# Eleven more w2 steps as seven block products: a gated mix of linear attention and an MLP on one core

## The chip, the core and the metric

The kernel runs on one core of one Trainium2 chip. The metric is the device time of one execution in microseconds (us); the three runs shown below took 1128.09 to 1129.79 us. The engines are named as in the profile: PE (matmuls; PEld are its weight loads), DVE (vector), ACT (scalar and activation), POOL (GpSimd) and SP, whose queue issues nearly all DMAs. PE and DVE/ACT meet in PSUM, 8 banks of 128 x 512 fp32.

## The reference

```python
def _A_ref(x, wqkv, wo):                 # linear attention, 32 heads of 18
    ...
    num = jnp.einsum("bhqd,bhde->bhqe", pq, kv)
    den = jnp.einsum("bhqd,bhd->bhq", pq, z)[..., None] + 1e-6
    o = num / den
    return (lambda x, *d: x.transpose(*d))(o, 0, 2, 1, 3).reshape(B, S, D) @ wo
def _B_ref(x, w1, b1, w2, b2):
    y = _layernorm(x, axis=-1)
    h = _gelu(jnp.einsum("bsd,df->bsf", y, w1) + b1)
    return jnp.einsum("bsf,fd->bsd", h, w2) + b2
g = _sigmoid((x * gate_w).sum(-1, keepdims=True))
return g * a + (1 - g) * b               # a = _A_ref(x, ...), b = _B_ref(x, ...)
```

There are S = 2048 tokens, D = 576 and F = 4608, all fp32.

## The kernel before

**Numbers as pairs.** fp32 values are split into a rounded part (type fp32r) and the rest, so that a product of two matrices is three products of parts: high x high, high x low, low x high. ACT makes the high part by a copy into fp32r, DVE the low part by a subtraction. Every split costs one instruction on ACT and then one on DVE.

**Stages.** First come q, k, v and the attention (to about 279 us in the trace), whose weighted result of the tokens 0 to 1023 stays in SBUF (`acc[0..7]`) and that of the tokens 1024 to 2047 goes to DRAM (`late_acc`). Then the MLP runs to the end in 36 steps, k = 0 to 35: 18 for the first 1024 tokens ("first half") and 18 for the others ("second half"). A step takes 256 of the 4608 hidden columns (two blocks f of 128) for 1024 tokens (two groups t of 512). The helper class `InOrder` records every instruction, so all of them carry its line in the profile, L109, and are told apart by their tiles.

**A step, part one: w1.** The product y @ w1 of a step is a 2 x 2 by 2 x 2 block product. It is made with Winograd's seven block products (`product`, tiles `y,wa` and `y,wb`), each of seven matmuls of 128 x 512; 49 matmuls per step. The PSUM banks X, Yb and Z hold sums of products. ACT copies X out (`kept`, u<-ps), DVE adds another bank (`plus`, u<-ps,u), ACT takes gelu twice (once rounded into `h`, once whole into `u`), DVE subtracts (h<-u,h). The w1 blocks and their sums are split in the first half (wa, wb, by ACT and DVE, the sums by POOL) and stored in DRAM (`w1d`); the second half loads them.

**A step, part two: w2.** h @ w2 of step k is done during the products of step k+1. In steps 0 to 17, 34 and 35 it is plain (`down`): eight tiles of 128 tokens, each 12 matmuls of 128 x 288 (two f, three terms, two halves of the columns) into a pair of PSUM banks; DVE then adds the pair, times 1-g, into the attention's result (accs<-ps,omg,accs). In steps 18 to 33 it is done with seven block products too (`unit`): 14 units of 6 matmuls of 128 x 288, each evicted by a DVE addition (accs<-ps,accs) into seven sums that are combined at the end. This asks for sums of h (`sum_h`, four POOL operations u<-u of 128 x 512, each split again by ACT and DVE) and sums of w2 blocks (`sum_w2`, four POOL operations fresh<-fresh of 128 x 288).

**What sets the order.** Each engine takes its instructions in program order. The order is written out by hand: one unit or tile of w2 behind each product or part of a product, with the splits at fixed places between them (`todo`, `later`). The units use two PSUM pairs in turn (`ff_pairs`, banks 6-7 and 4-5), so the unit after the next one waits until this one is evicted. Splitting y of the second half (tiles accs, region, yd) is spread over steps 1 to 15.

Of the kernel before, what the change touches and what calls it, by code (L numbers as in the profile page):

```python
# [17 lines left out]
P = 128  # L18
S, D, H, DH, F = 2048, 576, 32, 18, 4608
NT = S // P  # L20
# [49 lines left out]
A11, A12, S2, S1, A21, A22, S3, S4 = range(8)  # L70
FIRST_W, LAST_W = (A11, S1), (A22, S4)
# [6 lines left out]
PLAIN = 2 * NCHUNK - 2  # L78
LAST = 2 * NCHUNK - 1
DOWN_ORDER = (1, 4, 2, 5, 7, 6, 3)  # L80
W2_PLACES = [FACTORS[n][1] for n in DOWN_ORDER]
W2_GROUPS = ((0, 2), (2, 4), (4, 6), (6, 7))
# [30 lines left out]
def tile_gated_mix(ctx: ExitStack, tc: tile.TileContext, x, xm, xe, wm, we, wvm, wve, wo, um, ue, w2, b1, b2, gw, out):  # L113
# [39 lines left out]
    for _ in range(WARM):  # L153
# [11 lines left out]
    sums = {n: accs[:, i * TPB * HALF:(i + 1) * TPB * HALF].rearrange("p (s n) -> p s n", n=HALF)  # L165
            for i, n in enumerate(DOWN_ORDER)}
# [8 lines left out]
    mrt = keep.tile([2 * max(q1 - q0 for q0, q1 in MOMENTS), P], F32, name="mrt")  # L175
    moments = [dram.tile([2, (q1 - q0) * P], F32, name=f"moments{b}") for b, (q0, q1) in enumerate(MOMENTS)]
    w1d = [dram.tile([P, 7, 5, P], F32, name=f"w1d{c}") for c in range(NCHUNK)]
    late_acc = dram.tile([TPS, P, D], F32, name="late_acc")
# [203 lines left out]
    def store_moments(b, p):  # L382
        n = mr[b].shape[1] * mr[b].shape[2]
        act.activation(mrt[:n], p[:n], AF.Copy)
        sp.dma_start(moments[b].rearrange("a (t n) -> (a t) n", n=P), mrt[:n])
# [35 lines left out]
    def split_pair(sup, j, part, stage):  # L421
        m0, m1 = 2 * part, min(2 * part + 2, 7)
# [316 lines left out]
    for m in (B11, B21, T2, T1, T3, T4, B22):  # L739
        load_y(0, m)  # L740
# [15 lines left out]
    hs, c2s, w2raw = {}, {}, {}  # L756

    def wr(k):
        at_ = fresh[:, :24 * P] if k > 1 else spare[:, :24 * P]
        return at_.rearrange("p (m s n) -> p m s n", m=8, s=3)  # L760
# [9 lines left out]
    def sum_w1(k):  # L770
        r = wr(k)
        for to, x0, x1, op in ((S1, A21, A22, OP.add), (S2, S1, A11, OP.subtract), (S4, A12, S2, OP.subtract),
                               (S3, A11, A21, OP.subtract)):
            pool.tensor_tensor(out=r[:, to], in0=r[:, x0], in1=r[:, x1], op=op)

    def split_w1(k, first):

        a, b = FIRST_W if first else LAST_W
        b += 1
        w = wa if first else wb  # L780
        src = wr(k)[:, a:b]
        act.activation(w[:, :, 0:3], src, AF.Copy)
        dve.tensor_sub(w[:, :, 3:5], src[:, :, 0:2], raw(w[:, :, 0:2]))
        dve.tensor_sub(w[64:P, :, 2], src[64:P, :, 2], raw(w[64:P, :, 2]))
# [8 lines left out]
    def load_split_w1(k, a):  # L793
        place = a if a <= FIRST_W[1] else a - LAST_W[0] + 4
        sp.dma_start(raw(w1_of(a)).rearrange("p s n -> p (s n)"),
                     w1d[k % NCHUNK][:, place].rearrange("p s n -> p (s n)"))

    def w2_rows(k):
        c = k % NCHUNK
        return w2[c * CF * P:(c + 1) * CF * P].rearrange("(f p) d -> p f d", p=P)  # L800

    def load_w2(k, to):
        w2raw[k] = to.rearrange("p (f n) -> p f n", f=CF)
        sp.dma_start(w2raw[k], w2_rows(k))

    def split_w2(k, to, parts=(0, 1)):
        c2 = c2s[k] = to.rearrange("p (a f n) -> p a f n", a=2, f=CF)
        if 0 in parts:
            act.activation(c2[:, 0], w2raw[k], AF.Copy)
        if 1 in parts:  # L810
            dve.tensor_sub(c2[:, 1], w2raw[k], raw(c2[:, 0]))
# [19 lines left out]
    def plus(t, p):  # L831
        dve.tensor_tensor(out=t, in0=p, in1=t, op=OP.add)
        return t

    def gelu(k, f, t, src, whole, h=None, split=True):

        bias = b1s[:, k % NCHUNK * CF + f:k % NCHUNK * CF + f + 1]
        if split:
            h = hs[k, f, t] = take_h((k, f, t)) if h is None else h
            act.activation(h[:, 0], src, AF.Gelu_apprx_tanh, bias=bias)  # L840
        act.activation(whole, src, AF.Gelu_apprx_tanh, bias=bias)
        return lambda: dve.tensor_sub(h[:, 1], whole, raw(h[:, 0]))

    TERMS = ((0, 0), (0, 1), (1, 0))
    terms = [(f, a, w) for f in range(CF) for a, w in TERMS]

    def add(i, to, term):
        dve.scalar_tensor_tensor(to, term, omg[:, PLACE[i]:PLACE[i] + 1], to, op0=OP.mult, op1=OP.add)

    def down_terms(p, s, k, half, only=range(len(terms)), opens=True, closes=True):  # L850
        c0 = s % TPB * P
        for n in only:
            f, a, w = terms[n]
            pe.matmul(p, hs[k, f, s // TPB][:, a, c0:c0 + P], c2s[k][:, w, f, half_cols(half)],
                      start=opens and n == 0, stop=closes and n == len(terms) - 1)

    def down(k, s):

        if k >= 0:
            p = two_of(ff_pairs)[:, :, :HALF]  # L860
            for n in range(len(terms)):
                for half in range(2):
                    down_terms(p[:, half], s, k, half, (n,))
            if s % TPB == TPB - 1:
                give_back_h((k, 0, s // TPB), (k, 1, s // TPB))
            add(s, halves(acc[s]), p)
            if k == 1 + s:
                add(s, acc[s], b2b)
            if k == HALF_TIME - 1:
                sp.dma_start(out[s * P:(s + 1) * P, :], acc[s])  # L870
        for job in later.get((k + 1, s), ()):
            job()
# [3 lines left out]
    b2b = ffc.tile([P, D], F32, name="b2b")  # L876
    wa = ffc.tile([P, FIRST_W[1] - FIRST_W[0] + 1, 5, P], F32R, name="wa")
    wb = ffc.tile([P, LAST_W[1] - LAST_W[0] + 1, 5, P], F32R, name="wb")

# [4 lines left out]
    extra[3] += [lambda: sp.dma_start(b2b, everywhere(b2, D))]  # L884
    extra[5] += [lambda: sum_w1(0), lambda: act.activation(tiny, ones[:, 0:1], AF.Gelu_apprx_tanh)]
    extra[7] += [lambda: split_w1(0, True), lambda: store_w1(0, True)]
    extra[9] += [lambda: split_w1(0, False), lambda: load_w1(1), lambda: store_w1(0, False)]
    extra[11] += [lambda: sum_w1(1)]

# [18 lines left out]
    h_places = ctx.enter_context(tc.tile_pool(name="hp", bufs=1)).tile([P, 6, 2, SB], F32R, name="h")  # L908
    h_free, h_taken = list(range(6)), {}

    def take_h(key):
        h_taken[key] = h_free.pop(0)
        return h_places[:, h_taken[key]]
# [4 lines left out]
    up = ctx.enter_context(tc.tile_pool(name="up", bufs=6))  # L918


    fresh = ctx.enter_context(tc.tile_pool(name="fresh", bufs=1)).tile([P, 33 * P], F32, name="fresh")
    region = ctx.enter_context(tc.tile_pool(name="region", bufs=1)).tile([P, 56 * P], F32R, name="region")
    y_stage = [region[:, n * 10 * P:(n + 1) * 10 * P].rearrange("p (m s n) -> p m s n", m=2, s=5) for n in range(2)]
    w2_whole = fresh[:, 24 * P:33 * P]
    c2_places = [region[:, (20 + 18 * n) * P:(38 + 18 * n) * P] for n in range(2)]
    w2_sums = fresh[:, :7 * HALF].rearrange("p (m n) -> p m n", n=HALF)
# [310 lines left out]
```

## Time and profile before

| | |
|---|---|
| runs | 1129.5, 1129.79, 1128.09 us; median 1129.5 |
| span of the profiled execution | 1127.9 us |
| PE busy | 1116.1 us (99%), 6886 matmuls |
| DVE busy | 862.3 us (76%), 1292 instructions |
| ACT busy | 555.6 us (49%), 950 |
| POOL busy | 308.4 us (27%), 252 |
| DMA | 189.84 MB, mean 168 GB/s |

The profiled execution has no time of its own among the runs; its span, from the first to the last instruction, is 0.2 us below the fastest run and 1.6 us below the median. A row of a timeline gives start, duration, engine, line, operation, out<-in and shapes; matmuls overlap each other, so the pace of PE is read from one start to the next and not from the durations. A row of groups ends with busy time, mean duration in ns, and the idle time before the group with what ended it.

### The profile page before, as it was taken

The numbers are of one execution on the slowest core, as the hardware profiler recorded it, in microseconds if no ns is written. First come the engines' busy times: TensorE is split into PE (matmuls) and PEld (weight loads), VectorE is DVE, ScalarE is ACT, GpSimd is POOL, SyncE is SP. The second block draws the span as 40 slices with busy tenths as digits, with TensorE's granted clock in tenths as the row PEclk, the third lists the DMA queues.
The fourth block names the chain that finished last, engine by engine and source line by source line (L and its number), as shares of the span: only waits on it lengthen the run. The fifth ranks groups of instructions, "written<-read, shape, count | busy, mean of one in ns | idle before, by whom it ended". The sixth has DMA issues, their size and how long they took to land.

```text
span 1127.9 us, 18132 instructions
## 1 busy us (share of the span) xinstructions
PE 1116.1 (99%) x6886; PEld 1022.6 (91%) x6886; DVE 862.3 (76%) x1292; ACT 555.6 (49%) x950; POOL 308.4 (27%) x252
## 2 busy tenths in 40 slices
PE   9999999999999999999999999999999999999998
PEld 8999989999899999999999999988999899989988
DVE  4567775895669878778778765678899889888985
ACT  6667664443545444545444543455444544454441
POOL 2111112342111123112122111234453445344530
PEclk9999999999999999999999999999999999999999
DMA  6267854524454764555755549744444444444452
GB/s 183 58 112 262 174 165 185 232 93 144 172 168 171 230 220 155 210 168 191 241 190 175 189 165 385 292 134 121 123 136 136 122 121 136 136 120 123 137 174 84
DMA packets 102984, 189.84 MB, mean 168 GB/s; under 512 B 8300, under 2 KB 58748, under 8 KB 98674
## 3 DMA queue, kind: packets, MB, share of 16 engines
q1 hardware_dynamic: 102018, 187.94, 51.7%
q8 instruction: 54, 0.88, 0.3%
q10 hardware_dynamic: 720, 0.74, 0.2%
q14 instruction: 32, 0.26, 0.1%
q0 software_dynamic: 160, 0.01, 0.0%
HBM read 121.93 MB, written 66.73 MB: 167 GB/s over the span
## 4 chain that ended last, share of the span: by engine, by line
PE 87%; DVE 6%; ACT 3%; issue 2%; DMA 1%; SPq 0%; ACTq 0%; DVEq 0%
PE ps L109 87%; DVE den L109 1%; DVE accs L109 1%; DVE qt L109 1%; DVE region L109 1%; DVE acc L109 0%; DVE u L109 0%; DMA t<-in_xe 0%; DMA s<-in_we 0%; DMA s<-in_wm 0%; DVE y L109 0%; ACT L109 0%; ACT h L109 0%; ACT u L109 0%; SPq L109 0%
## 5 line engine op out<-in xcount | busy, mean ns | idle before, releaser
L109 PEld LDWEIGHTS ps<-region,h 128*128 128x128 f32 x2568 | 368.5, 188 | 23.1 <-DVE accs L109 1.0
L109 PE MATMUL ps<-region,h 128*128 128x288 f32 x2568 | 383.1, 295 | 0.9 <-DVE fresh L109 0.7
L109 PE MATMUL ps<-y,wa 128*128 128x512 f32 x1008 | 265.0, 392 | 0.0
L109 POOL TENSOR_TENSOR fresh<-fresh 128x384 f32<-128x384 f32 (+1 forms) x128 | 138.1, 1084 | 438.2 <-DMA fresh<-in_ue 175.0
L109 PE MATMUL ps<-y,wb 128*128 128x512 f32 x756 | 201.1, 395 | 1.0 <-ACT u L109 1.0
L109 PEld LDWEIGHTS ps<-y,wa 128*128 128x128 f32 x1008 | 177.8, 188 | 26.2
L109 DVE TENSOR_TENSOR accs<-ps,accs 128x576 f32<-128x576 f32 x210 | 158.0, 753 | 32.3 <-PE ps L109 22.7
L109 ACT ACTIVATE h<-u,b1s 128x512 fp32r<-128x512 f32 x90 | 65.3, 725 | 215.7 <-DVE u L109 215.7
L109 PEld LDWEIGHTS ps<-y,wb 128*128 128x128 f32 x756 | 132.9, 188 | 23.3 <-ACT u L109 1.7
L109 DVE SCALAR_TENSOR_TENSOR accs<-ps,omg,accs 128x576 f32<-128x576 f32 (+1 forms) x146 | 118.1, 810 | 45.0 <-PE ps L109 44.0
L109 ACT ACTIVATE u<-ps 128x512 f32<-128x512 f32 x108 | 63.8, 591 | 149.3 <-PE ps L109 149.0
L109 POOL TENSOR_TENSOR u<-u 128x512 f32<-128x512 f32 x64 | 100.2, 1566 | 126.0 <-ACT u L109 122.2
L109 PE MATMUL ps<-y 128*128 128x288 f32 (+1 forms) x896 | 126.5, 297 | 3.2 <-DVE acc L109 2.0
L109 PEld LDWEIGHTS ps<-y 128*128 128x128 f32 x896 | 122.2, 188 | 6.6 <-DVE acc L109 2.7
L109 DVE TENSOR_TENSOR h<-u,h 128x512 fp32r<-128x512 f32 x142 | 104.8, 738 | 27.3 <-ACT u L109 27.2
L109 ACT ACTIVATE u<-u,b1s 128x512 f32<-128x512 f32 x108 | 78.3, 725 | 53.9 <-DVE u L109 50.9
L109 DVE TENSOR_TENSOR u<-ps,u 128x512 f32<-128x512 f32 x108 | 74.2, 687 | 36.3 <-ACT u L109 23.3
L109 PEld LDWEIGHTS ps<-region 128*128 128x128 f32 x600 | 90.3, 188 | 8.9 <-ACT accs L109 0.5
L109 DVE TENSOR_TENSOR region<-fresh,region 128x576 fp32r<-128x576 f32 (+1 forms) x83 | 80.9, 975 | 20.7 <-ACT region L109 20.7
L109 PE MATMUL ps<-region 128*128 128x288 f32 x600 | 96.2, 295 | 0.1
L109 PE MATMUL ps<-wp,qt 128*128 128x288 f32 x448 | 63.6, 298 | 0.9 <-DVE qt L109 0.9
L109 PEld LDWEIGHTS ps<-wp,qt 128*128 128x128 f32 x448 | 59.9, 188 | 1.4 <-DVE qt L109 1.4
(136 smaller groups left out, 1056.2 us busy)
## 6 DMA issues: line engine op xcount, KB each, us to landing
w1d<-wa SPq DMA_DIRECT2D x18, 1280.0 KB
wa<-w1d SPq DMA_DIRECT2D x72, 320.0 KB
y<-yd SPq DMA_DIRECT2D x14, 1280.0 KB
w1d<-wb SPq DMA_DIRECT2D x18, 960.0 KB
wb<-w1d SPq DMA_DIRECT2D x54, 320.0 KB
fresh<-in_w SPq DMA_DIRECT2D x20, 576.0 KB
fresh<-in_w SPq DMA_DIRECT2D x32, 288.0 KB
fresh<-in_um SPq DMA_DIRECT2D x64, 128.0 KB
```

Of the source, the lines that this page charges most:

```text
L109: return lambda *args, **kwargs: self.tc.keep_in_program_order(op(*args, **kwargs))
```

## The change

- **Which steps.** The list `SEVEN` puts k = 1, 3, ..., 15 and 16 to 34 on seven block products for w2; 0, 2, ..., 14 and 35 stay plain. Before it was 18 to 33.
- **Added straight into the result.** The units run in the order 1, 2, 6, 5, 7, 3, 4 (`DOWN_ORDER`), for tokens q = 0 and then q = 1 of each group. Units 1, 2 and 5 open a PSUM pair; the others add onto what the pair already holds. Every unit is evicted by DVE with one addition into `acc8`, eight tiles of the result. There are no seven sums to combine. The factor 1-g is applied once for each tile at the end of each half (`finish_tile`), so the attention's result of the first half goes to DRAM too and is loaded again.
- **Plain steps.** A unit is 12 matmuls for two token tiles and one half of the columns. For token group t = 0 ACT copies the running result into the PSUM pair ahead of the matmuls (ps<-accs) and copies the pair out behind them (accs<-ps); for t = 1 DVE adds as before.
- **Products.** The order is 1, 5, 6, 2, 7, 4, 3, and ACT copies X into Yb inside PSUM (ps<-ps) so that product 2 adds onto it; one u<-ps copy and one DVE addition per step go.
- **Order.** Splits, sums, loads and y work are no longer at fixed places: each is put in a list with a due slot and an assumed duration (`Later`); 14 slots make a step. A job is emitted when the engine has credit by a model clock or when its slot is due. The units are emitted so that about three (`LAG`) are left over for the next step.

```diff
-DOWN_ORDER = (1, 4, 2, 5, 7, 6, 3)
+SLOTS = 14
+LAG = 3
+HOLD = 8
+SEVEN = {*range(1, NCHUNK - 2, 2), *range(NCHUNK - 2, LAST)}
+UP_ORDER = (1, 5, 6, 2, 7, 4, 3)
+DOWN_ORDER = (1, 2, 6, 5, 7, 3, 4)
+OPENS, TAKES = (1, 2, 5), (1, 6, 5, 4)
...
-        if i >= TPS:
-            sp.dma_start(late_acc[i - TPS], acc[i])
+        sp.dma_start(late_acc[i], acc[i])
...
+        def run(self, ns, most=2000):
+            self.credit = min(self.credit + ns, most)
+            while True:
+                able = [j for j in self.jobs if j[4]()]
+                if not able:
+                    return
+                j = min(able, key=lambda j: j[:2])
+                if self.credit <= 0 and j[0] > slot_of["now"]:
+                    return
+                self.jobs.remove(j)
+                self.credit -= j[2]
+                j[3]()
...
+    def dve_ns(cols):
+        return 155 + 1.04 * cols
+    def by_pool(cols, f, *args):
+        f(*args)
+        clock["pool"] = max(clock["now"], clock["pool"]) + 3 * cols
+        return after(clock["pool"] - clock["now"] + 400)
+    def run_slot():
+        ns = clock["now"] - clock["run"]
...
+        on_act.run(ns)
+        on_dve.run(ns)
+        slot_of["now"] += 1
...
+    def prepare_w1(k):
...
+        if k > 1:
+            load_w1(k)
+            landed = after(6500)
...
+    def prepare_w2(k):
+        if k > LAST:
+            return
+        load_w2(k)
...
+        when(after(4500), begin)
...
+        def prepare(self):
+            if self.pair is None:
+                self.pair = two_of(ff_pairs)[:, :, :HALF]
+                if self.seeded:
+                    act.activation(self.pair, self.start_of(), AF.Copy)
+                    on_act.charge(act_ns(2 * HALF))
+        def run(self):
+            (self.plain if self.n is None else self.one_of_seven)()
+            clock["now"] += self.count * 133
+            if self.seeded:
+                act.activation(self.to, self.pair, AF.Copy)
+                on_act.charge(act_ns(2 * HALF))
+                return
+            dve.tensor_tensor(out=self.to, in0=self.pair, in1=self.start_of(), op=OP.add)
+            on_dve.charge(753)
+        def one_of_seven(self):
...
+            opens = self.n in OPENS
+            for i, (x, y) in enumerate(TERMS):
+                for j in range(2):
+                    c0 = (2 * self.q + j) * P
+                    pe.matmul(self.pair[:, j], h[:, x, c0:c0 + P], w[:, y], start=opens and i == 0,
+                              stop=i == len(TERMS) - 1, skip_group_check=not opens)
...
+    def finish_tile(sup, s):
+        weighed(sup, s, attn[s], acc[s], attn[s])
+        if sup == 0:
+            sp.dma_start(out[s * P:(s + 1) * P, :], attn[s])
...
+                at = 2 * i + part
+                goal = 6 * LAG + work * (SLOTS - 1 - (at - 1 if at == HOLD else at)) / SLOTS
+                while queue and sum(u.count for u in queue[1:]) >= goal and queue[0].ready():
+                    do_unit()
+                run_slot()
```

On PE, where the program first differs in kind, the rows below are four products of step 3 of before with the w2 tiles between them (y,wa and y,wb are w1 products of 512 columns, region,h are w2 matmuls of 288).

```order
L109 MATMUL ps<-y,wb 128x512 x7
L109 MATMUL ps<-region,h 128x288 x12
L109 MATMUL ps<-y,wb 128x512 x7
L109 MATMUL ps<-region,h 128x288 x24
L109 MATMUL ps<-y,wa 128x512 x7
```

And these stand in step 4 of the change, which carries the seven-product units of k = 3.

```order
L118 MATMUL ps<-y,wa 128x512 x4
L118 MATMUL ps<-region,h 128x288 x6
L118 MATMUL ps<-y,wa 128x512 x3
L118 MATMUL ps<-region,h 128x288 x6
L118 MATMUL ps<-y,wb 128x512 x7
```

A piece of w2 is half as long and stands behind each part of a product; a step holds 84 w2 matmuls there instead of 96.

On DVE, a stretch of a second-half step of before (accs<-ps,accs are evictions, h<-u,h and region<-... are splits of h, sums of h and w2, u<-ps,u is `plus`):

```order
L109 TENSOR_TENSOR h<-u,h 128x512
L109 TENSOR_TENSOR region<-fresh,region 128x288
L109 TENSOR_TENSOR accs<-ps,accs 128x576
L109 TENSOR_TENSOR region<-u,region 128x512
L109 TENSOR_TENSOR accs<-ps,accs 128x576
L109 TENSOR_TENSOR region<-u,region 128x512
L109 TENSOR_TENSOR accs<-ps,accs 128x576
L109 TENSOR_TENSOR h<-u,h 128x512
L109 TENSOR_TENSOR accs<-ps,accs 128x576
```

The same part of a second-half step of the change:

```order
L118 TENSOR_TENSOR h<-u,h 128x512
L118 TENSOR_TENSOR region<-fresh,region 128x2x288
L118 TENSOR_TENSOR u<-ps,u 128x512
L118 TENSOR_TENSOR accs<-ps,accs 128x2x288 x2
L118 TENSOR_TENSOR region<-fresh,region 128x2x288
L118 TENSOR_TENSOR accs<-ps,accs 128x2x288
L118 TENSOR_TENSOR h<-u,h 128x512
L118 TENSOR_TENSOR accs<-ps,accs 128x2x288
L118 TENSOR_TENSOR h<-u,h 128x512 x2
L118 TENSOR_TENSOR region<-fresh,region 128x2x288
L118 TENSOR_TENSOR accs<-ps,accs 128x2x288
```

Splits that stood singly between evictions now stand in threes at two places of the step.

In the first half, DVE in the step that carries the units of k = 3 (ystage are splits of y for the second half):

```order
L118 TENSOR_TENSOR accs<-ps,accs 128x2x288
L118 TENSOR_TENSOR ystage<-accs,ystage 128x256
L118 TENSOR_TENSOR h<-u,h 128x512
L118 TENSOR_TENSOR accs<-ps,accs 128x2x288
L118 SCALAR_TENSOR_TENSOR ystage<-ystage,low_rows,accs 128x128
L118 TENSOR_TENSOR h<-u,h 128x512
L118 TENSOR_TENSOR region<-fresh,region 128x2x288
L118 TENSOR_TENSOR accs<-ps,accs 128x2x288 x2
L118 TENSOR_TENSOR h<-u,h 128x512
L118 TENSOR_TENSOR region<-fresh,region 128x288
L118 TENSOR_TENSOR accs<-ps,accs 128x2x288
```

and in the same place of before, where an eviction comes half as often:

```order
L109 SCALAR_TENSOR_TENSOR accs<-ps,omg,accs 128x576
L109 TENSOR_TENSOR accs<-accs 128x768
L109 TENSOR_TENSOR h<-u,h 128x512
L109 SCALAR_TENSOR_TENSOR accs<-ps,omg,accs 128x576
L109 TENSOR_TENSOR accs<-accs 128x768
L109 TENSOR_TENSOR wb<-fresh,wb 128x3x256
L109 TENSOR_TENSOR wb<-fresh,wb 64x3x128
L109 SCALAR_TENSOR_TENSOR accs<-ps,omg,accs 128x576
```

Beside the splits of w1, h and w2, which are there in both, the change puts 12 DVE evictions into such a step where before has eight.

More of the change, by code (lines that the diff above doesn't have):

```diff
@@ L832, in plus, with bias_of, split_all_w1 @@
         dve.tensor_tensor(out=t, in0=p, in1=t, op=OP.add)
[L833 to L872, printed above, removed]
+    def bias_of(k, f):
+        return b1s[:, k % NCHUNK * CF + f:k % NCHUNK * CF + f + 1]
     weigh(3)
     ffc = ctx.enter_context(tc.tile_pool(name="ffc", bufs=1))
-    b2b = ffc.tile([P, D], F32, name="b2b")
     wa = ffc.tile([P, FIRST_W[1] - FIRST_W[0] + 1, 5, P], F32R, name="wa")
     wb = ffc.tile([P, LAST_W[1] - LAST_W[0] + 1, 5, P], F32R, name="wb")
+    def split_all_w1(k, first):
+        a0, a1 = FIRST_W if first else LAST_W
+        for part in range(3):
+            split_w1(k, a0, a1 + 1, part)
     extra = {i: [] for i in range(NT)}
@@ L1154, in tile_gated_mix @@
         for i, n in enumerate(UP_ORDER):
             for part in range(2):
[L1156 removed]
+                assert not 0 < k < HALF_TIME or (k, "w1", FACTORS[n][0]) in done, (k, n)
+                product(k, n, into[n], n in (1, 5) or (n == 2 and not k), (range(0, 4), range(4, 7))[part])
+                clock["now"] += (4, 3)[part] * 230
                 if part:
+                    products_done.add((k, n))
                     finish_up(n)
[L1159 removed]
```

649 lines of the change are left out of this document (374 added, 275 removed).

## The prediction

> **What bounds the kernel now.** I read the page first: busy times, the granted clock in 40 slices, and the chain that ended last.
>
> ```profile
> PE 1116.1 (99%) x6886; PEld 1022.6 (91%) x6886; DVE 862.3 (76%) x1292; ACT 555.6 (49%) x950; POOL 308.4 (27%) x252
> ...
> PEclk9999999999999999999999999999999999999999
> ...
> PE 87%; DVE 6%; ACT 3%; issue 2%; DMA 1%; SPq 0%; ACTq 0%; DVEq 0%
> ```
>
> PE is busy for 99% of the span at the full clock and holds 87% of the chain. DVE is the next engine with 76%. A busy PE could still be waiting inside its pipeline, so I asked for PE's waits in the MLP, 293 us to the end:
>
> ```profile
> PE ps L109 <- DVE fresh L109: 0.7, 1, 0.7
> PE ps L109 <- ACT u L109: 0.3, 1, 0.3
> PE ps L109 <- DVE h L109: 0.2, 1, 0.2
> PE ps L109 <- DVE region L109: 0.2, 1, 0.2
> ```
>
> That is 1.4 us in 835. The time of the MLP is therefore the number of matmuls times their pace. The pace is read from one start to the next in PE's timeline, first in a plain step, then in a seven-product step:
>
> ```profile
> 315.76 1.77 PE L109 MATMUL ps<-y,wa 128*128 128x512 f32 x7
> 317.37 1.75 PE L109 MATMUL ps<-region,h 128*128 128x288 f32 x12
> 318.96 1.32 PE L109 MATMUL ps<-y,wa 128*128 128x512 f32 x5
> ...
> 339.72 0.63 PE L109 MATMUL ps<-y,wa 128*128 128x512 f32 x2
> ```
>
> ```profile
> 768.97 1.09 PE L109 MATMUL ps<-y,wa 128*128 128x512 f32 x4
> 769.90 0.95 PE L109 MATMUL ps<-region,h 128*128 128x288 f32 x6
> 770.69 0.86 PE L109 MATMUL ps<-y,wa 128*128 128x512 f32 x3
> ...
> 791.55 0.63 PE L109 MATMUL ps<-y,wa 128*128 128x512 f32 x2
> ```
>
> Seven of 512 take 1.61 us (0.230 each), twelve of 288 take 1.59 (0.1325 each). By count a plain step is 49 x 0.230 + 96 x 0.1325 = 24.0 us, and it took 339.72 - 315.76 = 23.96. A seven-product step is 49 x 0.230 + 84 x 0.1325 = 22.4, and it took 791.55 - 768.97 = 22.58.
>
> **What the change removes from PE.** Eleven steps go from 96 to 84 matmuls, 132 matmuls in all. At 0.1325 us that is 17.5 us; by the two measured steps it is 11 x 1.38 = 15.2. I take 17.5 and count waits apart. Nothing on PE is added. The profiled span of 1127.9 becomes 1110.4 if PE never waits longer than now. The median of the runs is 1.6 above that span, and I carry 1.6 over.
>
> **What it asks of DVE.** PE can keep its pace only if each unit is evicted before its PSUM pair is wanted again. The groups of the seven-product step above, DVE's own timeline, PE's timeline at one unit's end, and three windows give the prices:
>
> ```profile
> L109 DVE TENSOR_TENSOR accs<-ps,accs 128x576 f32<-128x576 f32 x14 | 10.5, 753 | 2.1 <-PE ps L109 1.5
> ...
> L109 POOL TENSOR_TENSOR u<-u 128x512 f32<-128x512 f32 x4 | 6.3, 1576 | 6.6 <-ACT u L109 6.4
> ...
> L109 DVE TENSOR_TENSOR h<-u,h 128x512 fp32r<-128x512 f32 x5 | 3.9, 780 | 0.0
> ```
>
> ```profile
> 803.09 0.76 DVE L109 TENSOR_TENSOR accs<-ps,accs 128x576 f32<-128x576 f32 x1
> 803.76 0.68 DVE L109 TENSOR_TENSOR region<-u,region 128x512 fp32r<-128x512 f32 x1
> ...
> 805.25 1.28 DVE L109 TENSOR_TENSOR h<-u,h 128x512 fp32r<-128x512 f32 x1
> ...
> 809.65 0.76 DVE L109 TENSOR_TENSOR accs<-ps,accs 128x576 f32<-128x576 f32 x1 [0.69 <-PE ps L109]
> ```
>
> ```profile
> 808.65 0.96 PE L109 MATMUL ps<-region 128*128 128x288 f32 x6
> 809.45 0.86 PE L109 MATMUL ps<-y,wb 128*128 128x512 f32 x3
> ```
>
> ```profile
> 340.00:364.00 24.00, 24.00 (x147) 21.93 (x146) 21.92 (x30) 11.70 (x16) 5.54 (x4) 1.00 0.48 160
> 676.00:700.00 24.00, 24.00 (x147) 21.92 (x146) 15.35 (x20) 9.39 (x13) 1.95 (x2) 1.00 1.00 380
> ...
> 814.00:837.00 23.00, 23.00 (x138) 20.74 (x137) 20.34 (x30) 10.67 (x18) 9.87 (x8) 1.00 0.43 127
> ```
>
> (The windows' columns are PE, PEld, DVE, ACT and POOL busy, clock, DMA share, GB/s.) An eviction of 576 columns takes 0.76 and the next instruction starts 0.67 behind it, so neighbours overlap by 0.08 to 0.09. It starts 0.2 behind its unit (809.65 against 809.45). A split of 512 takes 0.68 alone, so other widths are estimated at 0.15 us and 1.04 ns a column. Its worst row here is 1.28, and the h group's mean of 0.78 says that some are stretched, by 13% on average. POOL was running its sums in 9.87 of 23 us.
>
> [...]
>
> *Second half* (17 steps of 14 units). A step of the change has on DVE 14 evictions (10.5), 7 splits of h (4.8), 3 x 0.76 + 0.45 for w2 and two additions `plus` of 512 (1.4): 19.4 us, against 20.8 before (eight splits of 512, three `plus`). So DVE is not the bound there; 22.4 us are available. The order is what counts. Between the end of a unit and the next use of its pair PE has four matmuls of 512 (0.93), a unit (0.79) and three of 512 (0.69): 2.41 us. In the worst place of the order (two h splits and a w2 split between two evictions) DVE starts the first eviction 0.2 after its unit, and the second ends 0.67 + 0.61 + 0.61 + 0.67 + 0.76 = 3.32 later, 3.52 in all. The second unit ends at least 0.70 + 0.79 = 1.49 after the first, so its eviction ends 2.03 us behind it of 2.41 allowed: 0.4 us to spare, if POOL is quiet. Each split beside POOL costs up to 0.60 more. Two such places in 17 steps cost between nothing and, with three stretched splits, 1.4 us a step. I take 0.2 us a step, what one fully stretched split overruns the 0.4 by: **+3.4 us**.
>
> *First half* (8 steps that carry the units of k = 1, 3, ..., 15). There the splits of w1 and y come on top: 12 evictions by DVE (9.0), 6 splits of h (4.1), w2 2.7, `plus` 1.4, w1 3.7 (widths 512, 512, 768 and their tails 256, 256, 384), y 2.1 (three of 256 and of 128). The sum is 23.0 us in 36 instructions; 36 x 0.08 of overlap leave 20.1. Stretched by 13% of its 12.6 us of splits, it is 21.7 us against 23.2 of PE (half of a plain and a seven-product step, 46.4). Before, the fullest window had 21.92 in 24. DVE is at 94%, with little room to make up for a clump. In the order shown for the units of k = 3, the first three evictions with the y, h and w2 splits among them last 4.5 us, while the units end 3.2 apart. With 0.2 for the start the third ends 1.5 us behind its unit, of 2.41 allowed, and every split beside POOL and any lag from the rows ahead takes from the 0.9 that is left. The loss is between 0 and about 1.5 us a step; I take 0.5, **+4.0**. The plain steps between have 6 evictions and 17 us of DVE work and can wait for nothing.
>
> **ACT.** It gets 64 copies of 576 columns for the plain units. No row of PSUM preloading exists; priced like DVE's eviction (0.76) they are 49 us in 16 steps of 24, beside 11.7 in 24 now. A DVE unit of 12 matmuls (1.59) and a part of a product (0.69) lie between one seeded unit and the next in the same pair, 2.3 us, and the copy out and the preload behind it take 1.5. So I cost ACT at nothing; without that cover it would be up to 0.76 for each of 32 units.
>
> **Start and hand-over.** PE waits once at the first step, where product 4 needs ACT's copy of X:
>
> ```profile
> 285.49 1.77 PE L109 MATMUL ps<-y,wb 128*128 128x512 f32 x7
> 287.94 0.50 PE L109 MATMUL ps<-y,wb 128*128 128x512 f32 x1 [0.69 <-ACT u L109]
> ```
>
> In the change two w2 copies and half of the w1 copy stand ahead of that copy on ACT, with gelu behind it. By columns these are 0.7 each, and the copy that PE waits for may start up to 2 us later: between 0 and 2 more; I take **+1.0**. In the window at 676 us the DMA engines are full (share 1.00) with y and w1 of the second half. The change adds 2.3 MB of stored attention to load there, eight additions on DVE for the output, and w2 loads whose POOL sums wait in line: 0 to 5 us, I take **+0.8**. At the end 12.7 us of plain matmuls are left instead of 25, but the last w2 splits and the last gelu wait behind evictions; the 1 to 2 us that PE loses there now stay (-1.5 to +1.5, I take 0).
>
> Sum: 1110.4 + 3.4 + 4.0 + 1.0 + 0.8 = 1119.6 for the span, **1121** for the median.
>
> **Rivals.**
> - *DVE keeps up everywhere* (20%). For it: the plan charges each job 0.75 for 0.67 and spreads it; no window of before that was 91% full made PE wait. Against it: the threes in the order. Price: no waits beyond today's, 1110.4 + 1.6 = 1112.
> - *Most of the gain is eaten* (17%): the same waits at twice my price, 15 us, so 1127; it holds the part of "the same" (within 0.2%, 2.3 us, about what a measurement of this kernel can tell from no change).
> - *POOL and the threes decide: slower* (13%). POOL has 88 more sums, the four h sums of a step start near DVE's clump, and each split takes 1.28. Then PE waits about 0.8 us in each of the 17 late steps and 1.5 in the 8 early ones, 25.6 us: 1110.4 + 25.6 + 1.8 + 1.6 = 1139. It decides from 17.5 us of waits on. For it: the 1.28 row. Against it: POOL is busy for less than half of the time, and the mean split is 0.78.
> - *A split waits for the whole POOL instruction* (2% of the 13). A split that meets a sum would be held for up to 1.58, PE about 2 us a step in 25 steps: 1110.4 + 50 + 1.6 = 1162. [...] The rows speak against a full lock: 0.68 became 1.28, not 2.26.
> - That the matmuls don't fall is excluded: the order of PE shows 132 fewer.
>
> **How the numbers follow.** The forecast, 1115 to 1126, has 50%. The range from 1111.5 (no waits, a little recovered at the end) to 1130 leaves about 5% below and 13 to 15% above. Faster by over 0.2%: 20 + 50 + about 7 of the 17, so 77%; the same 10%; slower 13%.
>
> **What would show it.** Right: a second-half step is 22.5 to 22.8 us from one y,wa start to the next, and a pair of first-half steps 46.5 to 47.5 instead of 47.9; PE's waits name DVE accs. If DVE keeps up, these are 22.4 and 46.4 and no such row stands over 3 us. If POOL decides, DVE's h<-u,h has a mean near 1 us and steps of the second half reach 23.2. A wait of PE for ACT u of over 3 us in total would mean that I mis-sized ACT. What would make it wrong: DVE waiting in line for ACT or POOL inside the full steps, which the sums by busy time don't hold.

## The result, and the profile after

The changed kernel takes 1166.95 us (median of 4 runs, 1164.68 to 1167.56), the kernel before on the same chip 1129.64: a ratio of 1.033, with a 95% interval of 1.0316 to 1.0345. That is slower by 37 us. The forecast was 1121, the range ended at 1130.

The page of the profiled execution (span 1165.8 us) answers to the first lines shown of before:

```profile
PE 1118.5 (96%) x6754; PEld 1006.9 (86%) x6754; DVE 951.9 (82%) x1436; ACT 617.1 (53%) x1110; POOL 408.2 (35%) x337
...
PEclk9999999999999999999999999999999999999999
...
PE 70%; DVE 17%; DMA 5%; issue 3%; ACT 3%; SPq 1%; POOL 1%; DVEq 0%; POOLq 0%; ACTq 0%
```

PE has 132 matmuls fewer (6754 records against 6886) and is busy for 96% of a longer span. DVE holds 17% of the chain where it held 6%. PE's waits in the MLP, 293 us to the end, with us in total, times and the longest:

```profile
PE ps L118 <- DVE accs L118: 22.2, 29, 2.1
PE ps L118 <- ACT u L118: 12.0, 16, 1.8
PE ps L118 <- ACT h L118: 1.7, 2, 0.8
```

With the small rows these are 37 us; before they were 1.4. The rows don't hold the whole loss: PE is busy for 1118.5 us, and for 1099.3 in e1 below, which has the same matmuls. In part that is because a wait is some 0.16 us longer from start to start than its row says (an example follows), in part it is the clock (last section). A second-half step, in PE's timeline from one first `y,wa` matmul to the next:

```profile
794.33 1.09 PE L118 MATMUL ps<-y,wa 128*128 128x512 f32 x4
...
803.98 1.04 PE L118 MATMUL ps<-region,h 128*128 128x288 f32 x6 [0.68 <-ACT u L118]
...
817.67 1.09 PE L118 MATMUL ps<-y,wa 128*128 128x512 f32 x4
```

It takes 23.34 us; before it was 22.57, and the forecast said 22.5 to 22.8. There is one wait in it, of 0.68 by its row and of 0.84 in the starts, and the same one stands in each of the steps 21 to 34. The profile puts it down to ACT's u; but DVE's own timeline at that place, and POOL's, say something else:

```profile
799.45 0.76 DVE L118 TENSOR_TENSOR accs<-ps,accs 128x576 f32<-128x576 f32 x1 [0.20 <-PE ps L118]
800.12 1.28 DVE L118 TENSOR_TENSOR h<-u,h 128x512 fp32r<-128x512 f32 x2
801.32 1.85 DVE L118 TENSOR_TENSOR region<-fresh,region 128x576 fp32r<-128x576 f32 x1
803.09 0.74 DVE L118 TENSOR_TENSOR accs<-ps,accs 128x576 f32<-128x576 f32 x1
```

```profile
800.95 1.60 POOL L118 TENSOR_TENSOR u<-u 128x512 f32<-128x512 f32 x1 [4.91 <-DVE h L118]
```

Two h splits run undisturbed (1.28 for both). Then a w2 split starts while POOL's sum of h is under way, and takes 1.85 us in place of 0.75. The sum ends at 802.55 and the split at 803.17, 0.62 behind it: nearly the whole split is done after the sum. The eviction behind it ends at 803.83, and PE starts 0.15 later.

The steps of the first half fall into two kinds. The windows' columns are PE, PEld, DVE, ACT and POOL busy, clock, DMA share, GB/s; these are steps 12 and 13, and the second-half step from above:

```profile
566.90:593.50 26.60, 24.51 (x142) 20.98 (x141) 25.70 (x37) 16.34 (x28) 9.99 (x8) 1.00 0.54 192
593.50:616.50 23.00, 23.00 (x140) 20.97 (x140) 22.40 (x29) 13.88 (x23) 9.30 (x9) 1.00 0.43 141
794.30:817.60 23.30, 22.62 (x135) 20.17 (x134) 19.72 (x28) 10.67 (x18) 9.21 (x8) 1.00 0.68 227
```

Even steps (they run the seven products of the odd step before) take 26 to 30 us, step 12 with DVE busy all but 0.9 us; odd steps take 23.1 to 23.3 and PE waits for nothing in them. A wait of step 12 looks like that of the second half. DVE's, POOL's and PE's rows:

```profile
574.73 1.68 DVE L118 TENSOR_TENSOR h<-u,h 128x512 fp32r<-128x512 f32 x1
576.33 0.74 DVE L118 TENSOR_TENSOR accs<-ps,accs 128x576 f32<-128x576 f32 x1
```

```profile
574.26 1.60 POOL L118 TENSOR_TENSOR u<-u 128x512 f32<-128x512 f32 x1 [3.98 <-DVE h L118]
```

```profile
577.22 1.38 PE L118 MATMUL ps<-region,h 128*128 128x288 f32 x6 [0.59 <-DVE accs L118]
```

An h split takes 1.68 us in place of 0.68 and ends 0.55 behind POOL's sum; the eviction behind it ends at 577.07, and PE starts 0.15 later. The steps' times, from the same starts in PE's timeline, for both kernels and for those of the experiments (a dash where other steps than in the changed kernel have the seven products):

| kernel | even steps 2 to 16 | steps 17 to 20 | steps 21 to 34 | time, median |
|---|---|---|---|---|
| before | - | - | 316.0 | 1129.6 to 1130.2 |
| after | 220.4 | 100.6 | 327.1 | 1166.95 |
| e1, no sums | 191.1 | 91.1 | 313.8 | 1115.17 |
| e2, sums in pieces | 221.7 | 99.6 | 316.2 | 1157.03 |
| e4, no y sums | 206.9 | 101.5 | 327.3 | 1156.38 |
| e5, eviction first | 221.0 | 98.9 | 314.0 | 1154.1 |
| e6, sums aside | 219.1 | 99.8 | 329.7 | 1168.97 |
| e9, no w1 sums | 203.2 | 101.7 | 327.2 | 1150.88 |
| e10, no h sums in 2 to 15 | 207.4 | 101.4 | 326.9 | 1154.7 |
| e12, all plain units by ACT | 221.1 | 100.0 | 326.9 | 1169.97 |
| e11, late sevens | - | - | 314.0 | 1128.3 |

One of the four executions of e7, the profiled one, took 2787.66 us and is left out; e12 is the same kernel, profiled again.

### The profile page after: what moved, and what is told of

The parts are those of the page before. It is cut to its first block, busy times and chain, and to the rows that moved or that the text cites. A ratio compares the mean times of both kernels' runs of the same rounds, so it can differ in the third digit from the quotient of the medians.

```text
span 1165.8 us, 18634 instructions
## 1 busy us (share of the span) xinstructions
PE 1118.5 (96%) x6754; PEld 1006.9 (86%) x6754; DVE 951.9 (82%) x1436; ACT 617.1 (53%) x1110; POOL 408.2 (35%) x337
## 4 chain that ended last, share of the span: by engine, by line
PE 70%; DVE 17%; DMA 5%; issue 3%; ACT 3%; SPq 1%; POOL 1%; DVEq 0%; POOLq 0%; ACTq 0%
PE ps L118 70%; DVE accs L118 6%; DVE h L118 3%; DVE wa L118 2%; DVE region L118 2%; DMA fresh<-in_w 1%; DMA late_acc<-accs 1%; DVE wb L118 1%; ACT u L118 1%; DVE u L118 1%; SPq L118 1%; DMA t<-in_xe 1%; DVE den L118 1%; DMA accs<-in_xe 1%; DVE ystage L118 0%
## 5 line engine op out<-in xcount | busy, mean ns | idle before, releaser
L118 PEld LDWEIGHTS ps<-region,h 128*128 128x128 f32 x3132 | 458.2, 189 | 90.5 <-DVE accs L118 19.2
L118 PE MATMUL ps<-region,h 128*128 128x288 f32 x3132 | 492.6, 298 | 35.3 <-DVE accs L118 22.2
L118 DVE TENSOR_TENSOR accs<-ps,accs 128x576 f32<-128x576 f32 x398 | 295.6, 750 | 78.2 <-PE ps L118 72.6
L118 POOL TENSOR_TENSOR fresh<-fresh 128x288 f32<-128x288 f32 (+1 forms) x172 | 184.4, 1077 | 320.0 <-DMA fresh<-in_w 127.1
L118 POOL TENSOR_TENSOR u<-u 128x512 f32<-128x512 f32 x108 | 162.9, 1508 | 195.5 <-DVE h L118 131.0
L118 DVE TENSOR_TENSOR h<-u,h 128x512 fp32r<-128x512 f32 x225 | 183.8, 828 | 3.3 <-ACT u L118 1.5
L118 DVE TENSOR_TENSOR region<-fresh,region 128x576 fp32r<-128x576 f32 x126 | 112.3, 893 | 3.9 <-ACT region L118 3.9
L118 ACT ACTIVATE region<-fresh 128x576 fp32r<-128x576 f32 x126 | 77.3, 621 | 31.1 <-PE ps L118 26.4
L118 ACT ACTIVATE h<-u 128x512 fp32r<-128x512 f32 x108 | 66.0, 619 | 3.2 <-POOL u L118 3.1
L118 DVE TENSOR_TENSOR wa<-fresh,wa 128x512 fp32r<-128x512 f32 x64 | 51.9, 810 | 15.3 <-ACT wa L118 14.3
```

Of the source, the lines that this page charges most:

```text
L118: return lambda *args, **kwargs: self.tc.keep_in_program_order(op(*args, **kwargs))
```

## The experiments

My theory after the result: DVE's splits are held for whole POOL sums, and the evictions behind them come too late for the two PSUM pairs. The rivals: DVE has too much work by itself; the sums come late, and ACT and DVE wait for their results; the order of the units loses time whatever POOL does; ACT is late with the seeded units, those whose PSUM pair it fills ahead of the matmuls. The kernel before took 1129.9 to 1130.2 beside them.

**e1: no sums.** `sum_h`, `sum_w2` and `sum_w1` keep their places in the plan but issue nothing after the first steps, as here for h:

```diff
-        pool.tensor_tensor(out=wholes[(k, *to)], ...)
+        if k < 2:
+            pool.tensor_tensor(out=wholes[(k, *to)], ...)
```

> The kernel after, in the same order, with POOL's sums left out of the steps from 2 on (h, w2 and, from step 3 on, w1): the splits then take blocks that hold unsummed or older numbers, so the output is not the reference's. Theory (DVE's splits are held for whole POOL sums, and late evictions stop TensorE at the two PSUM pairs): the h splits (mean 0.83 us in the changed kernel) return to 0.68, a second-half step falls from 23.35 to 22.5-22.6 us, the even first-half steps lose most of their 2.1-4.8 us of waits, and the time is 1115 to 1130 us. Rival 1 (DVE has too many columns by itself in the even steps): the second half gains, the even steps still wait 2 us or more each; 1140 to 1150. Rival 2 (the order in which the units come, whatever POOL does): 1155 or more.

Measured: 1115.17 (1114.98 to 1115.23), ratio 0.9866 [0.9852, 0.9881]. 52 us go with POOL's sums, and all three parts of the table fall. DVE's groups over the MLP, first of the changed kernel, then of e1 (count, busy us and mean ns):

```profile
L118 DVE TENSOR_TENSOR accs<-ps,accs 128x576 f32<-128x576 f32 x398 | 295.6, 750 | 78.2 <-PE ps L118 72.6
L118 DVE TENSOR_TENSOR h<-u,h 128x512 fp32r<-128x512 f32 x225 | 183.8, 828 | 3.3 <-ACT u L118 1.5 <-ACT h L118 1.2
L118 DVE TENSOR_TENSOR region<-fresh,region 128x576 fp32r<-128x576 f32 x99 | 95.4, 966 | 3.9 <-ACT region L118 3.9
```

```profile
L118 DVE TENSOR_TENSOR accs<-ps,accs 128x576 f32<-128x576 f32 x398 | 297.2, 754 | 94.4 <-PE ps L118 88.9
L118 DVE TENSOR_TENSOR h<-u,h 128x512 fp32r<-128x512 f32 x225 | 152.6, 690 | 14.6 <-ACT u L118 14.2
L118 DVE TENSOR_TENSOR region<-fresh,region 128x576 fp32r<-128x576 f32 x99 | 74.2, 752 | 2.8 <-ACT region L118 2.8
```

The evictions, with one input in PSUM, are the same (a mean of 750 and 754 ns); the h splits lose 31 us, the w2 splits of 576 columns 21. The whole of DVE was busy for 951.9 us and is now for 863.0. The order of the units and ACT's copies for the seeded units are the same in e1, so neither makes the loss by itself. This run alone doesn't say whether PE lost its time to the holds or to waiting for the sums' results, since e1 takes both away.

**e6: sums aside.** The sums are made in the same places and sizes, but nobody uses them:

```diff
-        pool.tensor_tensor(out=wholes[(k, *to)], ...)
+        dst = aside if k > 1 else wholes[(k, *to)]
+        pool.tensor_tensor(out=dst, ...)
```

> The kernel after with POOL's sums still made, in the same sizes, from the same sources and in the same places of the order, but written (from step 2 on; w1's from step 3) to a tile that nobody reads; ACT and DVE split blocks that are not summed, so the output is not the reference's, and nobody waits for a sum's result. The tile takes the room of the ninth place of h, of which eight are ever taken. Theory (the port: DVE is held beside POOL): like the changed kernel, 1150 to 1167, the splits as long as there. Rival (the sums come late, and ACT and DVE wait for their results): like the kernel without sums (1115), 1115 to 1130.

Measured: 1168.97, ratio 1.0351 [1.0331, 1.037], 2 us above the range of the theory and far from the rival's. The whole loss is back with no one waiting for a sum, in every part of the table. Step 12 by its window:

```profile
567.00:593.50 26.50, 24.40 (x142) 21.00 (x141) 25.71 (x36) 16.36 (x28) 10.54 (x8) 1.00 0.52 187
```

DVE is busy for 25.71 us as in the changed kernel (25.70). In e1 the same step and the one behind it have

```profile
548.00:571.60 23.60, 23.59 (x141) 21.02 (x140) 20.61 (x36) 16.27 (x28) 0.00 (x0) 1.00 0.55 192
571.60:594.70 23.10, 23.10 (x141) 21.07 (x140) 20.05 (x33) 14.01 (x23) 0.00 (x0) 1.00 0.52 180
```

There DVE is busy for 20.61 us in step 12. So DVE's own work in an even step is 20.6 us of 23.2, as forecast (20.1), and POOL adds 5.1. In the odd step behind it POOL adds 2.3 (22.40 against 20.05) and costs PE nothing. The rival that the sums come late falls for the kernel as it is.

**e2: sums in pieces.** Each sum is cut along its columns: h in 4, w2 and w1 in 3:

```diff
-        pool.tensor_tensor(out=wholes[(k, *to)], ...)
+        for c in range(4):
+            cols = slice(c * P, (c + 1) * P)
+            pool.tensor_tensor(out=wholes[(k, *to)][:, cols], ...)
```

> The kernel after with each POOL sum cut in pieces along its columns: h in 4 of 128, w2 in 3 of 96, w1 in 3 of 128. All the work is done; POOL is busy for longer (an estimate from its three sizes, 0.31 us + 2.35 ns a column: 4 x 0.61 in place of 1.51 us). Theory, if a split waits for one POOL instruction to end: no split beside POOL takes more than 1.4 us (1.78 and 1.85 now), a second-half step takes 22.5-22.9 us; 1130 to 1150. Rival (a split and a POOL sum share a port by the column, so POOL's total time counts): the longest splits stay at 1.7 us or grow, 1165 to 1185.

Measured: 1157.03, ratio 1.0242 [1.0227, 1.0258], outside both ranges. The second half does what the theory says: 316.2 us in 14 steps, 22.59 each. At the place of the wait DVE's timeline has

```profile
801.10 1.28 DVE L118 TENSOR_TENSOR h<-u,h 128x512 fp32r<-128x512 f32 x2
802.30 1.02 DVE L118 TENSOR_TENSOR region<-fresh,region 128x576 fp32r<-128x576 f32 x1
803.24 0.75 DVE L118 TENSOR_TENSOR accs<-ps,accs 128x576 f32<-128x576 f32 x1
```

The split is held for one piece (it takes 1.02 in place of 0.75), although POOL works longer on the whole (3.01 us for the four pieces of this sum, 1.60 for the undivided one). The even steps gain nothing (221.7), and PE's waits in the MLP are named otherwise:

```profile
PE ps L118 <- DVE accs L118: 13.0, 21, 1.3
PE ps L118 <- ACT ps L118: 8.0, 4, 3.2
PE ps L118 <- DVE h L118: 5.1, 12, 0.7
```

ACT waits for a sum that is now later (2.12 us), and the copy of X into Yb (`ps<-ps`), which PE needs, is queued behind it. ACT's timeline:

```profile
574.90 0.64 ACT L118 ACTIVATE h<-u 128x512 fp32r<-128x512 f32 x1 [2.12 <-POOL u L118]
575.44 0.58 ACT L118 ACTIVATE ps<-ps 128x512 f32<-128x512 f32 x1
```

There a wait for a sum's result, which e6 excludes for the changed kernel, took the place of the hold. Sums in two pieces were not tried.

**e5: eviction first.** If the second half's loss is one split at one place, moving it behind the eviction ends it:

```diff
-            on_dve.add(due - 3, dve_ns(HALF * len(group)), low, next_slot())
+            then = slot_of["now"] + (seven and k >= NCHUNK - 2 and group[0] == 4)
+            on_dve.add(due - 3, dve_ns(HALF * len(group)), low, lambda: slot_of["now"] > then)
```

> The kernel after, all work done; from step 16 on one w2 split (the third group of a step) may be issued one slot later, so that DVE's eviction that stood behind it goes ahead of it. Theory (the loss of a second-half step is this one split, held 1.85 us in place of 0.75 by POOL's 1.60 us sum): a second-half step falls from 23.35 to 22.5-22.7 us, the first half is as before the edit, and the time is 1153 to 1158. Rival (POOL's sum holds whatever split comes next, or comes late itself, so the wait only moves): 1163 to 1169.

Measured: 1154.1, ratio 1.0211 [1.0196, 1.0226]. Steps 21 to 34 take 314.0 us, 22.43 each, and PE waits for nothing in them. DVE's timeline at the place:

```profile
799.65 1.28 DVE L118 TENSOR_TENSOR h<-u,h 128x512 fp32r<-128x512 f32 x2
800.85 0.75 DVE L118 TENSOR_TENSOR accs<-ps,accs 128x576 f32<-128x576 f32 x1
801.52 1.11 DVE L118 TENSOR_TENSOR h<-u,h 128x512 fp32r<-128x512 f32 x1
```

The eviction goes beside POOL's sum unharmed (0.75), and the h split behind it catches only the sum's rest (1.11). The edit doesn't touch ACT, and PE's waits for "ACT u" fall from 12.0 us (16 times) to

```profile
PE ps L118 <- ACT u L118: 2.5, 2, 1.8
```

So fourteen of those rows were DVE's late eviction, misnamed.

**e4, e9, e10: which work fills the even steps?** e4 leaves out DVE's normalising and differences of y, e9 POOL's sums of w1, e10 those of h in steps 2 to 15:

```diff
-        todo = [(on_dve, dve_ns(768), normal_pair, (1, j, n // 2, n % 2)) for n in range(4)]
-        todo += [(on_dve, dve_ns(384), sum_pair, (1, j, n)) for n in range(4)]
+        todo = [(on_dve, dve_ns(768), lambda *a: None, (1, j, n // 2, n % 2)) for n in range(4)]
+        todo += [(on_dve, dve_ns(384), lambda *a: None, (1, j, n)) for n in range(4)]
...
-            pool.tensor_tensor(out=r[:, to], in0=r[:, x0], in1=r[:, x1], op=op)
+            if k == 2:
+                pool.tensor_tensor(out=r[:, to], in0=r[:, x0], in1=r[:, x1], op=op)
...
-        pool.tensor_tensor(out=wholes[(k, *to)], ...)
+        if k < 2 or k >= NCHUNK - 2:
+            pool.tensor_tensor(out=wholes[(k, *to)], ...)
```

> The kernel after with 32 DVE instructions left out of the first half: the normalising and the differences of the second half's y (16 of 128x768, 16 of 128x384, some 28 us of DVE with their stretch), so the second half works on raw inputs and older blocks, and the output is not the reference's. Theory (POOL's holds of the splits at bad places): the even steps gain little, 1158 to 1166. Rival (DVE's own load in the even steps): they gain what is taken from DVE, 1140 to 1152.

> The kernel after without POOL's w1 sums from step 3 on (the splits take older blocks, so the output is not the reference's); the h and w2 sums stay. In the changed kernel's trace the even steps of the first half hold DVE's splits for 2.2 to 5.8 us each beyond their length alone, 0.8 to 2.2 of it beside w1 sums, 1.4 to 3.2 beside h sums. Theory (in these steps DVE has no time to spare, so every held microsecond is one of TensorE): the even steps get 0.8 to 2.2 us shorter, the second half stays at 23.35 a step; 1151 to 1160. Rival (only the h sums, which come beside the h splits, matter; or the order of the units alone): 1163 to 1168.

> The kernel after without POOL's sums of h in the steps 2 to 15 (the splits take unsummed blocks, so the output is not the reference's); the w1 and w2 sums stay, and so does the second half. Theory (every held microsecond of the even steps counts): they get 1.4 to 3.2 us shorter each, 1145 to 1155, and the second half stays at 23.35 a step. Rival (the w1 sums make the loss): 1160 or more.

Measured: 1156.38 for e4 (ratio 1.023 [1.0213, 1.0247]), 1150.88 for e9 (1.0188 [1.0175, 1.0202]), 1154.7 for e10 (1.0226 [1.0212, 1.024]). e9 and e10 go as the theory says (e9 is 0.1 us below its range): the even steps get 17.2 and 12.9 us shorter, the rest stays. Together that is slightly more than the 29.3 us of e1, so the two are not shares of one sum. e4 lies between the two ranges: the even steps gain 13.5 us for some 28 us of DVE work taken away over the half, more than I allowed. In these three, relief of an even step helps, be it a held microsecond or a worked one. A balance fits step 12: DVE's work leaves 2.6 us of such a step's 23.2 free, POOL's holds need 5.1, and the step is 2.9 us longer than in e1. It is argued from busy times, and the next run shows that it isn't the whole account.

**e7 and e12: all plain units by ACT.** ACT takes evictions over from DVE:

```diff
-            self.seeded = n is None and t == 0
+            self.seeded = n is None
```

> The kernel after with all plain units of the first half preloaded into PSUM and evicted by ACT (the changed kernel: half of them); all work done. DVE loses some 37 evictions of 0.75 us, ACT gains as many pairs of 2 x 0.65 us. Rival (DVE's own load decides the first half): 1140 to 1152. Theory (a split held beside POOL at the wrong place decides): these units run mostly in the odd steps, which have no waits, so the gain is small, 1156 to 1167; if ACT comes late by it, 1170.

> The kernel with all plain units preloaded and evicted by ACT, looked at again for a profile of an undisturbed execution: 1170 to 1173 as in the other runs of e7_all_seeded. Theory (DVE's splits, held by POOL, decide the even steps, and ACT now comes later as well): the even steps still wait for DVE, and waits for ACT's results in the first half grow beyond the changed kernel's 12.7 us of waits for u. Rival (DVE's load decides): the even steps' waits for DVE fall by the 37 evictions taken away.

Measured: 1171.37 for e7 (ratio 1.0364 [1.0347, 1.0382]), 1169.97 for e12 (1.0352 [1.0313, 1.0391]), both above the theory's 1156 to 1167 and near the 1170 that I gave for a late ACT. DVE has 32 instructions fewer than in the changed kernel (1404 against 1436; I had counted on some 37), the even steps take 221.1 us against 220.4, and PE's waits for DVE accs are 25.8 us against 22.2. The rival of DVE's load falls in this form. PE's waits for ACT u didn't grow (10.9 us against 12.7 over the MLP), but most of those rows are misnamed, as e5 shows. DVE's own waits say that ACT did come later; its h splits waited for ACT u for 1.5 us in the changed kernel (row above), and here

```profile
L118 DVE TENSOR_TENSOR h<-u,h 128x512 fp32r<-128x512 f32 x225 | 182.0, 820 | 12.7 <-ACT u L118 10.9 <-ACT h L118 1.2
```

Step 12 of e12 shows that a full DVE is not what it takes:

```profile
565.70:593.60 27.90, 25.46 (x140) 22.21 (x140) 22.99 (x34) 17.80 (x30) 8.48 (x7) 0.94 0.43 154
```

DVE is idle for 4.9 us of it, and PE still waits for DVE's evictions twice, 2.4 us in all. Whether the late ACT makes the 3 to 4 us by which the time is longer isn't settled.

**e3: plain first half, and e8: the old set of sevens.**

```diff
-SEVEN = {*range(1, NCHUNK - 2, 2), *range(NCHUNK - 2, LAST)}
+SEVEN = {*range(NCHUNK - 2, LAST)}
```

```diff
-SEVEN = {*range(1, NCHUNK - 2, 2), *range(NCHUNK - 2, LAST)}
+SEVEN = {*range(NCHUNK, LAST - 1)}
```

> The kernel after with the seven block products in steps 16 to 34 alone; steps 1, 3, ... 15 plain again. If the first half's seven products cost more than they save (the pairs of steps take 49-53 us, two plain ones by TensorE's own work 48.0), the steps 1 to 17 take 410 us in place of 427, and the time is 1145 to 1155. If they pay after all, and the loss lies in the second half and at the hand-over alone: 1175 to 1180.

> The changed kernel's planner, order of the products and preloads by ACT, but with the seven block products in the steps where the kernel before had them (18 to 33); all work done. If the eleven more steps make the loss, it goes: 1126 to 1132. If the new order makes the second half's wait by itself: 0.8 us in each of 15 steps, 1136 to 1143.

Measured: 1144.47 for e3, ratio 1.0127 [1.0112, 1.0142], 0.5 below its range of 1145 to 1155. Its steps 1 to 17 take 405.7 us against 427.5, so the eight sevens of the first half cost 21.8 us on balance. e8 has 1140.95, ratio 1.0096 [1.0079, 1.0113], in the range of the new order. With the steps 17 and 34 plain it leaves out the 16 blends at the ends of the halves and the store of the first half's rows, so it does not do all the work, as I had said it would. Its matmuls are as many as before's, its plain steps take 23.80 (before 23.95), and yet the steps 20 to 34 take 23.35 to 23.37 with one wait of the same 0.84, start to start, in each. So the new order, with POOL's sums beside it, makes the second half's loss without one seven more.

**e11: a version made of these.** Sevens in steps 18 to 34, e5's edit, and the finishing of the first half's rows one per slot:

```diff
-SEVEN = {*range(1, NCHUNK - 2, 2), *range(NCHUNK - 2, LAST)}
+SEVEN = {*range(NCHUNK, LAST)}
...
+                on_dve.add(now + 1 + n, 814, lambda s=s: finish_tile(u.k // NCHUNK, s),
+                           next_slot() if u.n else lambda n=n: slot_of["now"] > now + n)
```

> A candidate, all work done: the changed kernel's planner with seven products only in steps 18 to 34 (one more than the kernel before), the one w2 split of the second half behind the next eviction, and the finishing of the first half's rows spread over the slots of step 18. By the steps of the runs so far (plain 23.80, second half 22.43, 26.4 for step 2, 39.7 for the last): 12.5 + 21.6 + 26.4 + 16 x 23.85 + 23.2 + 15 x 22.45 + 39.7 = 842 us in place of 845.0, and 1125 to 1129. If finishing the rows beside a full DVE stops TensorE: up to 1132.

Measured: 1128.3 (1127.69 to 1129.39, 11 runs), ratio 0.9988 [0.9979, 0.9997]. It is ahead of the kernel before by 1.8 us, hardly more than can be told from nothing, and ahead of the changed one by 39. PE waits 5.5 us in its MLP:

```profile
PE ps L118 <- DVE accs L118: 2.1, 5, 0.8
PE ps L118 <- ACT u L118: 1.8, 2, 1.6
PE ps L118 <- ACT ps L118: 0.9, 1, 0.9
PE ps L118 <- issue: 0.7, 1, 0.7
```

## Why the prediction was wrong

- **The matmuls removed (-17.5): right.** Without the sums, steps 21 to 34 run at 22.41 each, the count's 22.4.
- **Second half (+0.2 a step): the step that failed first.** The place was right, two h splits and a w2 split between two evictions. The sizes were not: I let each split lose "up to 0.60" beside POOL. The runs show a w2 split held for 1.10 there, 0.95 us a step against e1 (13.4 us in 14 steps). The 0.60 came from the row of 1.28 in before's trace, which I set against a POOL sum of 1.58 and read as a partial hold ("0.68 became 1.28, not 2.26"). POOL's own timeline of before at that moment, which the prediction doesn't show, has a short sum:

```profile
805.18 0.80 POOL L109 TENSOR_TENSOR fresh<-fresh 128x288 f32<-128x288 f32 x1 [5.56 <-DMA fresh<-in_w]
```

  The split started at 805.25, the sum ended at 805.98, the split at 806.53: it was held for the whole of a 0.80 sum. Before's trace has a longer one, too. DVE's and POOL's rows:

```profile
1074.64 2.27 DVE L109 TENSOR_TENSOR region<-u,region 128x512 fp32r<-128x512 f32 x1
```

```profile
1073.31 3.05 POOL L109 TENSOR_TENSOR accs<-accs 128x1152 f32<-128x1152 f32 x1 [2.82 <-DVE accs L109]
```

  Here the sum ends at 1076.36 and the split at 1076.91. In all these places a split ends 0.55 (512 columns) to 0.62 (576) behind the sum, whatever the sum's length (0.80 to 3.05). The pieces of e2 agree: there the split waits for one piece, not for the four. I had such a hold at 2%. What in the chip makes it, a port as the expectations of e2 and e6 suppose, no run shows.
- **First half (+0.5 for each of 8 even steps): mis-sized by seven times.** DVE's own load was right (20.1 forecast, 20.6 in e1's row). The hold was put at 13% of 12.6 us of splits, 1.6 us; it is 5.1 in step 12. The 13% was the mean of five h splits in one second-half step of before; it was used for a step in which POOL has sums of h and w1 beside an almost full DVE. Against e1 the even steps cost 29.3 us, 3.7 each. In the steps 2, 6 and 10 up to 1.7 us of it (an estimate, last section) is the clock at half behind a wait, for which the prediction has no term.
- **Hand-over (+0.8): too small.** The steps 17 to 20 cost 9.4 us against e1, and e6 has nearly all of it again (99.8 us), so it hangs on POOL's sums. What part late w2 loads have in it was not tried.
- **ACT (0) and the end (0).** Nearly all the waits named for ACT u were DVE's. From its first matmul to the start of the last, step 35 takes 40.49 us against 39.55 in e1 (0.9 more) and 39.00 before: 1.5, the edge of the range for the end. The start was mis-priced the other way, step 0 takes 12.51 against 12.19 before (+0.3 of +1.0).
- **Rivals.** "POOL and the threes decide" (1139) named the mechanism, and its 0.8 a late step is close to the 0.95. It had the early steps at 1.5 against 3.7. "A split waits for the whole POOL instruction" (1162) has the hold that these rows show; that it is near the time is in part luck, for it has 2 us in each of 25 steps, where 0.95 and 3.7 were measured. Of the signs that I named for POOL, second-half steps at 23.2 came (23.34), a mean of h<-u,h near 1 us did not (0.83): it is not the mean that counts but where the held split stands.

The sum against e1 closes: 29.3 + 9.4 + 13.4 + 0.9 = 53.0 us, and the MLPs differ by 53.3.

## What to carry to other kernels

A split's price beside POOL was not a percentage here: in the places shown the split ended 0.55 to 0.62 us behind the POOL instruction, which made it 1.10 us longer in the second-half step and 1.00 in step 12. So I would first try the rest of the POOL instruction that runs when the split comes up as the price, and ask at each clump which POOL instruction its own producer has just set free (here the h split started the sum that held the split behind it). What a hold costs couldn't be read from the engine's busy share: step 13, with DVE busy for 22.40 of 23.0 us, lost nothing, and a second-half step, with 19.72 of 23.3, lost 0.95. So follow each held split to the eviction behind it and to the PSUM pair that this frees. The eviction, which reads PSUM, took 0.75 beside POOL's sum in e5; put ahead of the split, it brought a second-half step from 23.34 us to 22.43. Cutting the POOL instruction shortened the hold in e2 (the split took 1.02 in place of 1.85), but it made the result later (ACT waited 2.12 us for it).

## What the runs showed of the hardware

TensorE's clock fell behind a wait of 1.81 us. PE's timeline in step 10, and three windows of it:

```profile
520.88 1.86 PE L118 MATMUL ps<-region,h 128*128 128x288 f32 x12 [1.72 <-DVE accs L118]
...
528.55 1.04 PE L118 MATMUL ps<-region,h 128*128 128x288 f32 x6 [1.81 <-DVE accs L118]
529.43 1.83 PE L118 MATMUL ps<-y,wa 128*128 128x512 f32 x4
531.05 1.65 PE L118 MATMUL ps<-region,h 128*128 128x288 f32 x6
532.49 1.07 PE L118 MATMUL ps<-y,wa 128*128 128x512 f32 x3
```

```profile
519.30:522.70 3.40, 1.82 (x13) 1.82 (x14) 3.40 (x6) 2.71 (x5) 1.27 (x1) 1.00 0.88 364
526.10:529.50 3.40, 1.59 (x10) 1.17 (x9) 3.40 (x4) 1.11 (x2) 1.09 (x1) 1.00 0.65 196
529.50:532.90 3.40, 3.40 (x12) 2.96 (x11) 2.87 (x7) 0.00 (x0) 0.00 (x0) 0.50 0.83 302
```

Behind the second wait four matmuls of 512 take 1.62 us from start to start (0.92 otherwise) and six of 288 1.44 (0.80), and the granted clock is 0.50 for 3.4 us. In the 3.4 us before, PE was busy for 1.59; around the first wait, of 1.72, it was busy for 1.82, and the clock stayed at 1.00. A second-half step with its single wait of 0.68 keeps 1.00 too. The clock is at half in four such stretches of the trace (from 331.5, 427.1, 529.5 and 730.9, in the steps 2, 6, 10 and 18), and 3.4 us at half the clock set back a busy PE by 1.7, so all four by some 7 of the 37 us (an estimate). Why one wait was followed by the half clock and the other was not, no run shows.
